# Four row transfers without waits between them, and gate dots at another rate

## The chip, the core and the metric

The kernel runs on one core of a Trainium2 chip. The metric is the device time of one execution in microseconds (us), so lower is better. The core has five engines, each with its own instruction stream: PE (TensorE, matmuls), ACT (ScalarE), DVE (VectorE), POOL (GpSimd) and SP (SyncE, which here only issues DMAs). An instruction can wait on semaphores that other engines or landed DMAs raise; everything behind it on its engine then waits too.

## The reference

Three stages follow one another. With S = 3072, D = 256 and 8 batches there are 24,576 tokens.

```
scores = z @ z.T / S;  attn = max(scores, 0)**2;  x = u * (attn @ v)           # attention, per batch
h = x @ w_in;  g = h * clip(h + 3, 0, 6) / 6;  x = g @ w_out                   # first MLP, d_ff = 2048
logits = x @ w_gate;  e = argmax(logits);  gate = softmax(logits)[e]           # routing, 8 experts
out = gate * sigmoid(x @ w_output_gate)[e] * (max(x @ w1[e], 0) @ w2[e])       # one expert of 8 per token
```

## The kernel before

Tokens are worked in 48 chunks q of 512, six (`NC`) to a batch. Each chunk passes an **A** block (attention: 24 units, one per 128 keys, `NJ`), and later an **M** block (first MLP: 16 units, one per 128 hidden features, `NF`). Blocks alternate: M(4), A(6), M(5), A(7) and so on up to M(45), A(47), then the M blocks that are left, then the experts (`E` units). All float32 products are made of high and low halves, so that one product is three matmuls.

The order is written out by hand. `run` walks over the units; for unit n it issues the scores or the first MLP matmul of a unit some places ahead (`stage1`), the split into halves two units ahead (`stage2`), and then `back`, the second matmul, which sums into the four PSUM banks `psx`. `when(step, fn)` hangs a side job on a step, behind that step's matmuls. A program step is no time: each engine runs its own list as far as its waits allow.

What matters here is what happens at the end of an M block. Its result for 512 tokens (four groups s of 128) stands in the four banks `psx`. The next block's `back` needs these banks, so PE may go on only after `evacuate` (ACT line 429, then DVE line 430) has copied each bank to `row[:, s]` in SBUF. There is one `row` tile for all chunks of this phase. During the next A and M blocks the chunk in `row` is routed: 32 **gate dots** on DVE (line 445, one per group and expert), the four `route` stages (lines 382 to 425; stage 4 ends with line 425), and then four **scatters** on POOL (line 434), indirect DMAs that send each token's row of 260 floats to its expert's region in HBM, `xs_d`. Only when scatter s has landed may the next chunk's `evacuate` write `row[:, s]`. `xs_d` is one tile, and each scatter counts as a write of the whole of it, so a scatter also waits until the one before it has landed.

`plan_chunk` sets the steps. m1 is the last unit of M(q), so the A block behind it spans m1+1 to m1+24 and the M block after that m1+25 to m1+40. Of a chunk with an A block behind it, `na` dots go into the A block at `ra` per unit, the rest into the following M block (line 677). n is the step behind the last dot; route stage 4 and the scatters stand at n+4. Chunks with (q+3) divisible by 6 have 26 dots in the A block, the others 18. The chunk's successor is evacuated behind m1+40. Of the chunks 4 to 45, which have an A block behind them, seven are of the 26-dot kind (9, 15, ..., 45).

On POOL, besides scatters, two subtractions per chunk (line 309, `xlt`, the low half of the MLP's input) run in the A block; in the expert phase POOL adds (line 636) and scatters results to `out` (line 639).

Of the kernel before, what the change touches and what calls it, by code (L numbers as in the profile page):

```python
# [8 lines left out]
F32 = mybir.dt.float32  # L9
# [18 lines left out]
def kernel(  # L28
# [17 lines left out]
    E = wcat.shape[0]  # L46
# [3 lines left out]
    NJ = S // P  # L50
    NF = DFF // P
    NC = S // TC
    NQ = B * NC
    NSUB = TC // P
# [15 lines left out]
    pe, act, dve, pool, sp = nc.tensor, nc.scalar, nc.vector, nc.gpsimd, nc.sync  # L70
# [6 lines left out]
    const = ctx.enter_context(tc.tile_pool(name="const", bufs=1))  # L77
# [9 lines left out]
    ident = const.tile([P, P], F32, name="ident")  # L87
    tri = const.tile([P, P], BF16, name="tri")
    ones = const.tile([P, P], BF16, name="ones")
    three = const.tile([P, 1], F32, name="three")  # L90
    ebias = const.tile([P, 1], F32, name="ebias")
    gbc = const.tile([P, E, D], F32, name="gbc")
# [54 lines left out]
    def when(step, fn, early=False):  # L147
        bg.setdefault((max(step, low[0]), not early), []).append(fn)
# [6 lines left out]
    def load_z(b, t):  # L155
        zr = ap.tile([P, TC], F32, tag="stage", name="zr", bufs=5)
        for h in range(2):
            sp.dma_start(out=zr[h * DQ:(h + 1) * DQ], in_=zT[b, :, t * TC:(t + 1) * TC])
        zraw[b, t] = zr
# [22 lines left out]
    def load_u(q):  # L182
        b, c = divmod(q, NC)
        t = mp.tile([P, ND, TC], F32, tag="xu", name="xut", bufs=2)
        sp.dma_start(out=t, in_=uT[b, :, c * TC:(c + 1) * TC].rearrange("(d p) t -> p d t", p=P))
        xu[q] = t
# [95 lines left out]
    def sum_o(q, d):  # L282
        if halves(q):
            t = ap.tile([P, TC], F32, tag="os", name="os", bufs=2)
            act.copy(t, o_t[q][2 * d + 1])  # L285
            dve.tensor_add(t, t, o_t[q][2 * d])
            osum[q, d] = t
        else:
            osum[q, d] = o_t[q][d]
            mul_x(q, d)  # L290

    def mul_x(q, d):
        if (q, d) in osum:
            dve.tensor_mul(xu[q][:, d, :], xu[q][:, d, :], osum.pop((q, d)))

    def split_x(q, d):
        if q in alt:
            if d == 0:
                alt[q] = pools["e"].tile([P, 2, ND, TC], F32R, tag="ws", name="xat", bufs=NPAIR + 2)
            h, l = (alt[q][:, k, d, :] for k in range(2))  # L300
        else:
            h = mp.tile([P, TC], F32R, tag="xph", name="xht", bufs=ND)
            l = mp.tile([P, TC], F32R, tag="xpl", name="xlt", bufs=ND)
        act.copy(h, xu[q][:, d, :])
        xh.setdefault(q, []).append(h)
        xl.setdefault(q, []).append(l)

    def split_xl(q, d):
        pool.tensor_sub(xl[q][d], xu[q][:, d, :], xh[q][d].bitcast(F32))

    def save_x(q):
        sp.dma_start(out=xsave[q], in_=xu.pop(q).rearrange("p d t -> p (d t)"))

    def reload_x(q):
        t = mp.tile([P, ND, TC], F32, tag="xu", name="xut", bufs=2)
        sp.dma_start(out=t, in_=xsave[q].rearrange("p (d t) -> p d t", d=ND))
        xu[q] = t
# [61 lines left out]
    def row_of(q):  # L379
        return pools["row"] if q in alt else row0  # L380
# [46 lines left out]
    def evacuate(q, s):  # L427
        o, row = o_t["x", q], row_of(q)
        act.activation(row[:, s, :D], o[s][:, :D], AF.Copy, scale=1.0 / 6.0)  # L429
        dve.scalar_tensor_tensor(row[:, s, :D], o[s][:, D:], 1.0 / 6.0, row[:, s, :D],  # L430
                                 op0=ALU.mult, op1=ALU.add)

    def scatter(q, s):
        pool.indirect_dma_start(  # L434
            out=xs_d,
            out_offset=bass.IndirectOffsetOnAxis(ap=rt["di", q][:, s:s + 1], axis=0),
            in_=row_of(q)[:, s, :],
            in_offset=None,
        )

    def gate_dot(q, k):
        s, e = divmod(k, E)
        if k == 0:
            rt["lg"] = rtile("lg", [P, NSUB, E])
        dve.tensor_tensor_reduce(junk, row_of(q)[:, s, :D], gbc[:, e, :], 1.0, 0.0, op0=ALU.mult, op1=ALU.add,  # L445
                                 accum_out=rt["lg"][:, s, e:e + 1])
# [50 lines left out]
    def table2a(stage):  # L497
        m, n, w = small["m"], stile("n2", 2 * E), stile("c")
        if stage == 0:
            ceil_div(n[:, E:], SLOT - 1)  # L500
        elif stage == 1:
            dve.tensor_sub(n[:, E:], n[:, E:], m[:, :E])
            p = prefix(n)
            dve.tensor_copy(tail[:, :E], base[0:1, :])
            dve.tensor_copy(tail[:, E:], p[0:1, 2 * E - 1:])
        elif stage == 2:
            dve.tensor_sub(w, m[:, :E], m[:, 1:])
            dve.tensor_add(w, w, n[:, E:])
        else:
            place(small["pa"], w, m[:, 0:1])  # L510

    def tableb(i):
        se = small["se"]
        w = TW[i]
        ps = ps_a()
        for j in range(2):
            mm(ps[0:1, j * w:(j + 1) * w], se[:, j:j + 1], ident[:, :w], True, True)
        dve.tensor_copy(tab[i][:, :2 * w], ps[0:1, :2 * w])
        dve.memset(tab[i][:, 2 * w:2 * w + 1], 1)
        dve.tensor_tensor(tab[i][:, 2 * w + 1:], tab[i][:, w + 1:2 * w], tab[i][:, w:2 * w - 1], op=ALU.not_equal)  # L520

    def fill_tail(e):
        r = nc.values_load(tail[0:1, e:e + 1], engines=(mybir.EngineType.SP,),
                           min_val=e * REG, max_val=e * REG + NT)
        sp.dma_start(out=xs_d[bass.ds(r, SLOT), :].rearrange("(a p) c -> p a c", p=P), in_=zrow)
# [131 lines left out]
    def plan_chunk(q):  # L657
        b, c = divmod(q, NC)
        s0, e0 = at["A", q, 0], at["A", q, NJ - 1]
        m0, m1 = at["M", q, 0], at["M", q, NF - 1]  # L660
        if q > 1:
            when(s0 + 4, lambda: load_u(q))
        for d in range(ND):
            when(e0 + 1, lambda d=d: sum_o(q, d))
            when(e0 + 2 + d, lambda d=d: mul_x(q, d))
        if q < NSAVE:
            when(e0 + 5, lambda: save_x(q))
            when(m0 - NF - 8, lambda: reload_x(q))
        sx = m0 - NF + 4 if q < NSAVE or q == NQ - 1 else m0 - NJ + 2
        for d in range(ND):  # L670
            when(sx + 2 * d, lambda d=d: split_x(q, d))
            when(sx + 2 * d + 1, lambda d=d: split_xl(q, d))
        kind = order[m1 + 1][0]
        if kind == "A":
            na, ra = (18, 0.85) if (q + 3) % NC else (26, 1.2)
            dots = [m1 + 2 + int(k / ra) for k in range(na)]
            dots += [m1 + NJ + 1 + int(k / 1.7) for k in range(NSUB * E - na)]
        else:
            rate = {"M": 3.0 if q else 1.0, "E": 0.5}[kind]
            d0 = m1 + 2 if kind != "E" else m1 + 22  # L680
            dots = [d0 + int(k / rate) for k in range(NSUB * E)]
        for k, step in enumerate(dots):
            when(step, lambda k=k: gate_dot(q, k))
        n = dots[-1] + 1
        for s in range(NSUB):
            when(m1 + 1, lambda s=s: evacuate(q, s))
        for st in range(1, 5):
            when(n + st - (st == 1), lambda st=st: route(q, st))
        sc = n + 4
        if q < NLATE:  # L690
            E0 = at["E", 0, 0]
            sc = max(E0 + 1, sc + (E0 + 1 - sc) % NPAIR)
        for st in range(NSUB):
            when(sc + (st * NPAIR if q < NLATE else 0), lambda st=st: scatter(q, st))
        if q == 1:
            for st in range(4):
                when(n + 6 + st, lambda st=st: table2a(st))
            when(n + 11, lambda: tableb(1))
            for e in range(E):
                when(sc + NPAIR * (NSUB + e), lambda e=e: fill_tail(e))  # L700
        if c == NC - 1 and b + 1 < B:
            for t in range(NZ):
                at_z = e0 + 1 + (5 * t) // 2
                when(at_z - 4, lambda t=t: load_z(b + 1, t))
                when(at_z, lambda t=t: prep_z(b + 1, t))
            for i in range(NV):
                at_v = e0 + 2 + (6 * i) // 5
                when(at_v - 3, lambda i=i: load_v(b + 1, i))
                when(at_v, lambda i=i: prep_v(b + 1, i))

    for q in range(NQ):
        plan_chunk(q)
# [152 lines left out]
```

## Time and profile before

| | |
|---|---|
| median of 3 runs | 5595.7 us (5592.58 to 5596.53) |
| profiled execution | 5592.97 us, its span 5590.8 us |
| PE busy | 5477.0 us (98%) |
| DVE busy | 4307.9 us (77%) |
| ACT busy | 3462.8 us (62%) |
| POOL busy | 904.1 us (16%) |
| mean granted TensorE clock | 0.989 |

PE is busy nearly all the time, so what counts is each stretch in which it stands still or runs slowly. Matmuls overlap in the trace (one of 512 columns shows some 400 ns, and starts follow one another every 230 ns or so), so a full-speed stretch and a half-speed stretch both look busy; the granted clock tells them apart.

### The profile page before, as it was taken

To read this page: it belongs to the slowest core of one execution; us is meant where nothing else is said; L and a number is where in the kernel's file an instruction comes from. 1 tells how busy PE (TensorE), PEld (TensorE's weight loads), DVE (VectorE), ACT (ScalarE), POOL (GpSimd) and SP (SyncE) were. 2 spreads that over 40 slices of the span, in tenths; PEclk is the share of its full clock that TensorE was granted. 3 is DMA by queue.
4 is the path that set the end of the run, shared out by engine and by line. 5 is a ranking of instruction groups with operands and counts; after the bars stand their busy time and mean duration, and the time that the engine had idled before them with its cause. 6 is when DMAs were issued, how large, how long until landed. Compare 5 with 4: busy or idle time off the path is not lost.

```text
span 5590.8 us, 97495 instructions
## 1 busy us (share of the span) xinstructions
PE 5477.0 (98%) x35672; PEld 4636.9 (83%) x35672; DVE 4307.9 (77%) x9967; ACT 3462.8 (62%) x5993; POOL 904.1 (16%) x782
## 2 busy tenths in 40 slices
PE   9999999999999999999999999999999999999999
PEld 6788778878887888788877888887888899999998
DVE  8977777777777777777777777777768888888887
ACT  7765566556655665565556555655554677777776
POOL 3200001000100000000000000100011244444443
PEclk9999999999999999999999999999999999999999
DMA  3110001000100000010001000100000122222233
GB/s 95 57 37 12 12 22 41 9 23 18 33 9 26 27 23 9 26 37 12 11 23 37 13 12 22 41 9 16 9 18 18 56 76 82 80 73 73 80 114 111
DMA packets 127381, 209.42 MB, mean 37 GB/s; under 512 B 15389, under 2 KB 84766, under 8 KB 126752
## 3 DMA queue, kind: packets, MB, share of 16 engines
q1 hardware_dynamic: 108064, 152.26, 9.4%
q0 software_dynamic: 18816, 50.75, 2.5%
q8 instruction: 281, 4.60, 0.3%
q14 instruction: 220, 1.80, 0.1%
HBM read 147.73 MB, written 56.27 MB: 36 GB/s over the span
## 4 chain that ended last, share of the span: by engine, by line
PE 75%; issue 12%; POOL 6%; DMA 4%; DVE 2%; ACT 1%; POOLq 0%; ACTq 0%; SPq 0%; DVEq 0%
PE psx L197 48%; PE psa L197 27%; POOL out L639 4%; DMA xs_d<-row,r_di 4%; POOL yt L636 1%; POOL xs_d L434 1%; DVE wst L581 0%; DVE row L430 0%; DVE lot L243 0%; ACT gt L231 0%; DVE gt L232 0%; ACT row L429 0%; PE psa L588 0%; DVE lot L611 0%; DVE junk L445 0%
## 5 line engine op out<-in xcount | busy, mean ns | idle before, releaser
L197 PE MATMUL psx<-hit,vht 64*128 64x512 f32 (+1 forms) x4320 | 1421.3, 403 | 91.6 <-DVE row L430 91.1
L197 PE MATMUL psx<-lot,vht 64*128 64x512 f32 (+1 forms) x4320 | 1413.0, 403 | 0.9 <-DVE lot L243 0.7
L197 PE MATMUL psx<-hit,vlt 64*128 64x512 f32 (+1 forms) x4320 | 1406.8, 402 | 0.0
L197 PE MATMUL psx<-wo,hit 128*128 128x512 f32 x3072 | 1114.0, 398 | 0.0
L231 ACT ACTIVATE gt<-psa,three 128x512 f32<-128x512 f32 x768 | 529.3, 689 | 890.2 <-PE psa L197 884.7
L197 PE MATMUL psa<-xht,win 128*128 128x512 f32 x2880 | 998.6, 394 | 0.0
L197 PEld LDWEIGHTS psx<-hit,vht 64*128 64x128 f32 (+1 forms) x4320 | 814.0, 189 | 221.6 <-DVE row L430 117.5
L219 ACT ACTIVATE at<-psa 128x512 f32<-128x512 f32 x1152 | 679.8, 590 | 375.9 <-PE psa L197 351.6
L243 DVE TENSOR_TENSOR lot<-at,hit 128x512 fp32r<-128x512 f32 x1152 | 816.2, 709 | 117.5 <-ACT hit L242 74.0
L197 PEld LDWEIGHTS psx<-hit,vlt 64*128 64x128 f32 (+1 forms) x4320 | 815.8, 190 | 92.2
L197 PEld LDWEIGHTS psx<-lot,vht 64*128 64x128 f32 (+1 forms) x4320 | 812.9, 190 | 85.7 <-DVE lot L243 2.0
L232 DVE SCALAR_TENSOR_TENSOR gt<-gt,psa 128x512 f32<-128x512 f32 x768 | 527.1, 686 | 443.2 <-ACT gt L231 430.5
L197 PE MATMUL psx<-wo,lot 128*128 128x256 f32 x3072 | 860.4, 280 | 0.0
L220 ACT ACTIVATE at<-at 128x512 f32<-128x512 f32 x1152 | 728.9, 633 | 36.7
L445 DVE CUSTOM_DVE_ANT_0 junk<-row,gbc 128x256 f32<-128x256 f32 x1536 | 736.3, 479 | 12.1
L434 POOL DMA_INDIRECT xs_d<-row,r_di x192 | 202.7, 1056 | 3297.3 <-DVE row L425 2955.5
L197 PEld LDWEIGHTS psx<-wo,hit 128*128 128x128 f32 x3072 | 577.0, 188 | 150.8 <-ACT at L219 15.5
L197 PEld LDWEIGHTS psa<-xht,win 128*128 128x128 f32 x2880 | 540.9, 188 | 138.0 <-ACT os L285 12.4
L197 PE MATMUL psa<-xht,wst 128*128 128x256 f32 x3200 | 649.7, 284 | 4.1 <-DVE wst L581 4.1
L197 PEld LDWEIGHTS psx<-wo,lot 128*128 128x128 f32 x3072 | 579.5, 189 | 25.4 <-DVE lot L243 0.4
L243 DVE TENSOR_TENSOR lot<-gt,hit 128x512 fp32r<-128x512 f32 x768 | 528.3, 688 | 83.4 <-ACT hit L242 83.4
L197 PE MATMUL psx<-wst,hit 128*128 128x512 f32 x1600 | 578.1, 395 | 0.0
(141 smaller groups left out, 9608.2 us busy)
## 6 DMA issues: line engine op xcount, KB each, us to landing
w<-in_wcat SPq DMA_DIRECT2D x64, 512.0 KB
x<-xs_d SPq DMA_DIRECT2D x100, 260.0 KB
vr<-in_v SPq DMA_DIRECT2D x96, 256.0 KB
xut<-in_uT SPq DMA_DIRECT2D x48, 512.0 KB
ogt<-in_w_ogT SPq DMA_DIRECT2D x100, 128.0 KB
zr<-in_zT SPq DMA_DIRECT2D x96, 128.0 KB
wraw<-in_w_in SPq DMA_DIRECT2D x16, 256.0 KB
wraw<-in_w_out SPq DMA_DIRECT2D x16, 256.0 KB
```

Source lines behind the costliest of these rows:

```text
L197: pe.matmul(o, l, r, start=start, stop=stop)
L219: act.activation(t, ps, AF.Relu, scale=1.0 / S)
L220: act.activation(t, t, AF.Square)
L231: act.activation(t, ps, AF.Relu, bias=three)
L232: dve.scalar_tensor_tensor(t, t, 6.0, ps, op0=ALU.min, op1=ALU.mult)
L243: dve.tensor_sub(l, t, h.bitcast(F32))
L434: pool.indirect_dma_start(out=xs_d, out_offset=bass.IndirectOffsetOnAxis(ap=rt["di", q][:, s:s + 1], axis=0), in_=row_of(q)[:, s, :], in_o ...
L445: dve.tensor_tensor_reduce(junk, row_of(q)[:, s, :D], gbc[:, e, :], 1.0, 0.0, op0=ALU.mult, op1=ALU.add, accum_out=rt["lg"][:, s, e:e + 1])
L636: pool.tensor_add(y[:, 0, :], y[:, 0, :], y[:, 1, :])
L639: ins = pool.indirect_dma_start(out=out, out_offset=bass.IndirectOffsetOnAxis(ap=x.bitcast(I32)[:, s, D + 1:D + 2], axis=0), in_=y[:, 0, : ...
```

## The change

Two edits. The scatter is put in a group of writers of `xs_d` that do not depend on one another, and a memset of one element on POOL stands before each. The dots of chunks of the 18-dot kind go 20 into the A block at 0.95 per unit; the rest of both kinds starts one unit later in the M block and goes 2.2 per unit instead of 1.7.

```diff
+    spacer = const.tile([1, 1], F32, name="spacer")
...
     def scatter(q, s):
-        pool.indirect_dma_start(
+        pool.memset(spacer, 0.0)
+        ins = pool.indirect_dma_start(
             out=xs_d,
             out_offset=bass.IndirectOffsetOnAxis(ap=rt["di", q][:, s:s + 1], axis=0),
             in_=row_of(q)[:, s, :],
             in_offset=None,
-        )
+        ).ins
+        tc.declare_no_dep(ins, group="xs", reason="each token has a row of its own")
+        tc.add_to_no_dep_group("xs", ins)
...
-            na, ra = (18, 0.85) if (q + 3) % NC else (26, 1.2)
+            na, ra = (20, 0.95) if (q + 3) % NC else (26, 1.2)
             dots = [m1 + 2 + int(k / ra) for k in range(na)]
-            dots += [m1 + NJ + 1 + int(k / 1.7) for k in range(NSUB * E - na)]
+            dots += [m1 + NJ + 2 + int(k / 2.2) for k in range(NSUB * E - na)]
```

On POOL, the four scatters of one chunk and the subtractions behind them stood like this before (a `DMASW` name is a semaphore that landed indirect DMAs raise, eight of them in turn; `DVE_49` is DVE's):

```order
L434 DMA xs_d<-row_82,r_di 198912x260 [waits DMASW3_49,DVE_49]
L434 DMA xs_d<-row_82,r_di 198912x260 [waits DMASW4_49]
L434 DMA xs_d<-row_82,r_di 198912x260 [waits DMASW5_49]
L434 DMA xs_d<-row_82,r_di 198912x260 [waits DMASW6_49]
L309 TENSOR_TENSOR xlt<-xut,xht 128x512 [waits DMAHW5_49,PE_49,Activation_49]
```

and stand like this now (lines are one to four numbers higher, and `row_83` is the same tile):

```order
L435 MEMSET spacer 1x1 [waits Pool_49]
L436 DMA xs_d<-row_83,r_di 198912x260 [waits DMASW0_49,DVE_49]
L435 MEMSET spacer 1x1 [waits Pool_49]
L436 DMA xs_d<-row_83,r_di 198912x260 [waits DMASW1_49]
L435 MEMSET spacer 1x1 [waits Pool_49]
L436 DMA xs_d<-row_83,r_di 198912x260 [waits DMASW2_49]
L435 MEMSET spacer 1x1 [waits Pool_49]
L436 DMA xs_d<-row_83,r_di 198912x260 [waits DMASW3_49]
L310 TENSOR_TENSOR xlt<-xut,xht 128x512 [waits DMAHW0_49,PE_49,Activation_49]
```

Before, each scatter waited for the semaphore of the scatter just ahead of it. Now the semaphore it waits for is its own, which the scatter eight places ahead (two chunks earlier) raised; the first eight scatters of the program, which have none ahead, carry no such wait.

On DVE, the end of an M block stood like this before, from route stage 4 (`r_sm`, then line 425) to the first split of the next block (`hit<-at`); a `gt`, `lot` pair is one M unit:

```order
L232 SCALAR_TENSOR_TENSOR gt<-gt,psa 128x512
L243 TENSOR_TENSOR lot<-gt,hit 128x512
L424 TENSOR_REDUCE r_sm<-r_d 128x4
L425 TENSOR_SCALAR row_82<-r_sm 128x4
L232 SCALAR_TENSOR_TENSOR gt<-gt,psa 128x512
L243 TENSOR_TENSOR lot<-gt,hit 128x512 x2
L240 CAST hit<-at 128x512
```

and now:

```order
L233 SCALAR_TENSOR_TENSOR gt<-gt,psa 128x512
L244 TENSOR_TENSOR lot<-gt,hit 128x512
L425 TENSOR_REDUCE r_sm<-r_d 128x4
L426 TENSOR_SCALAR row_83<-r_sm 128x4
L233 SCALAR_TENSOR_TENSOR gt<-gt,psa 128x512
L244 TENSOR_TENSOR lot<-gt,hit 128x512
L233 SCALAR_TENSOR_TENSOR gt<-gt,psa 128x512
L244 TENSOR_TENSOR lot<-gt,hit 128x512 x2
L241 CAST hit<-at 128x512
```

Route stage 4, which releases the scatters, has moved ahead by one M unit in chunks of the 18-dot kind. In the seven chunks of the 26-dot kind it moves back by one, since their last dot goes from step m1+27 to m1+28. In the expert phase nothing moves but the memsets ahead of the eight scatters of chunks 0 and 1.

## Rows read from the trace of the kernel before

**Rows 1.** The page's busy time by engine: us, share of the span, instructions.

```profile
PE 5477.0 (98%) x35672; PEld 4636.9 (83%) x35672; DVE 4307.9 (77%) x9967; ACT 3462.8 (62%) x5993; POOL 904.1 (16%) x782
```

**Rows 2.** Groups by line and form: busy us, mean ns | idle us before, releasers.

```profile
L197 PE MATMUL psx<-hit,vht 64*128 64x512 f32 x4032 | 1303.5, 402 | 91.1 <-DVE row L430 91.1
```

**Rows 3.** Waits: waiter <- waited for: us in total, times, longest.

```profile
POOL xs_d L434 <- DMA xs_d<-row,r_di: 248.1, 122, 3.8
...
ACT row L429 <- DMA xs_d<-row,r_di: 115.7, 59, 2.9
...
PE psx L197 <- DVE row L430: 91.1, 62, 2.8
```

**Rows 4.** Timeline of POOL at M(13)'s end: start, us, what, [idle before <- releaser].

```profile
1137.34 0.99 POOL L434 DMA_INDIRECT xs_d<-row,r_di  x1 [72.51 <-DVE row L425]
...
1142.92 1.37 POOL L434 DMA_INDIRECT xs_d<-row,r_di  x1 [1.76 <-DMA xs_d<-row,r_di]
1146.72 0.96 POOL L434 DMA_INDIRECT xs_d<-row,r_di  x1 [2.43 <-DMA xs_d<-row,r_di]
```

**Rows 5.** Timeline of ACT, the same place: first two and last evacuation.

```profile
1143.90 0.75 ACT L429 ACTIVATE row<-psx 128x256 f32<-128x256 f32 x2
...
1149.25 0.38 ACT L429 ACTIVATE row<-psx 128x256 f32<-128x256 f32 x1 [2.33 <-DMA xs_d<-row,r_di]
```

**Rows 6.** Timeline of PE, the same place: its two pauses.

```profile
1147.43 0.49 PE L197 MATMUL psx<-hit,vht 64*128 64x512 f32 x1 [0.91 <-DVE row L430]
1150.15 0.79 PE L197 MATMUL psx<-hit,vht 64*128 64x512 f32 x1 [2.22 <-DVE row L430]
```

**Rows 7.** Timeline of POOL before M(10)'s end: last scatter of chunk 9 (26-dot kind).

```profile
863.87 1.45 POOL L434 DMA_INDIRECT xs_d<-row,r_di  x1 [2.64 <-PE psa L197]
```

**Rows 8.** Timeline of ACT at M(10)'s end: its four evacuations.

```profile
871.46 1.19 ACT L429 ACTIVATE row<-psx 128x256 f32<-128x256 f32 x4
```

**Rows 9.** Windows: stretch: us, busy us (x) of PE, PEld, DVE, ACT, POOL, PEclk, DMA.

```profile
1150.00:1156.40 6.40, 6.25 (x30) 4.92 (x32) 6.19 (x15) 4.62 (x9) 1.28 (x1) 0.52 0.00 0
1156.40:1175.00 18.60, 18.60 (x164) 15.97 (x162) 14.88 (x40) 12.86 (x23) 1.29 (x1) 1.00 0.11 30
```

**Rows 10.** The core's span and its mean granted TensorE clock.

```profile
core 0: 5590.8 us, clock 0.989
```

**Rows 11.** Timeline of PE: first scores behind M(5), M(10), M(11), M(45).

```profile
412.18 0.50 PE L197 MATMUL psa<-zht 64*128 64x512 f32 x2
...
871.97 0.50 PE L197 MATMUL psa<-zht 64*128 64x512 f32 x2
...
959.83 0.50 PE L197 MATMUL psa<-zht 64*128 64x512 f32 x2
...
4076.97 0.50 PE L197 MATMUL psa<-zht 64*128 64x512 f32 x2
```

**Rows 12.** Timeline of POOL: the program's last scatter, right behind another.

```profile
5581.74 0.98 POOL L639 DMA_INDIRECT out<-yt,x  x1 [0.30 <-issue]
```

**Rows 13.** Groups by line and form: a gate dot; a memset of 128x8.

```profile
L445 DVE CUSTOM_DVE_ANT_0 junk<-row,gbc 128x256 f32<-128x256 f32 x1536 | 736.3, 479 | 12.1
...
L654 POOL MEMSET row<- 128x8 f32 x1 | 0.1, 103 | 0.0
```

**Rows 14.** Timeline of DVE late in M(13): two successive units.

```profile
1135.47 0.69 DVE L232 SCALAR_TENSOR_TENSOR gt<-gt,psa 128x512 f32<-128x512 f32 x1 [0.81 <-ACT gt L231]
...
1138.26 0.69 DVE L232 SCALAR_TENSOR_TENSOR gt<-gt,psa 128x512 f32<-128x512 f32 x1 [1.19 <-ACT gt L231]
```

**Rows 15.** Timeline of all engines in A(12), unit 5: POOL's subtraction, a dot, `lot`, its matmul.

```profile
878.47 1.37 POOL L309 TENSOR_TENSOR xlt<-xut,xht 128x512 fp32r<-128x512 f32 x1 [1.14 <-ACT xht L304]
...
878.61 1.52 DVE L445 CUSTOM_DVE_ANT_0 junk<-row,gbc 128x256 f32<-128x256 f32 x1
...
880.50 0.69 DVE L243 TENSOR_TENSOR lot<-at,hit 128x512 fp32r<-128x512 f32 x1
...
881.53 0.39 PE L197 MATMUL psx<-lot,vht 64*128 64x512 f32 x1
```

## The prediction

> **What bounds the kernel now.** I read the page's busy times first: PE is at 98%, the next engine at 77% [rows 1], so time can come only from PE's idle stretches or from stretches in which it runs slowly. The groups by line show where PE idles: of some 114 us (span less busy time), 91.1 lie in front of one group, the matmuls that begin an A block's `back`, and all of it ends with DVE line 430, the evacuation of the block before [rows 2]. The list of waits gives the chain behind it: that matmul waits for DVE line 430, whose ACT partner, line 429, waits 59 times, 115.7 us in all, for a scatter to land, and a scatter waits 122 times, 248.1 us, 2.03 on the mean, for the scatter ahead of it [rows 3].
>
> The timeline shows one case, the end of M(13), where chunk 12 is scattered. The first scatter starts at 1137.34, when route stage 4 releases it. The others each wait some 1.8 to 2.4 us for the landing of the one ahead, so the last starts at 1146.72 and ends at 1147.68 [rows 4]. ACT evacuates groups 0 and 1 at 1143.90, but group 3 only at 1149.25, 2.33 us late, when that scatter has landed [rows 5]. PE pauses 0.91 and then 2.22 us [rows 6].
>
> Where the scatters are early, nothing pauses: chunk 9, with 26 dots in its A block, issues its last one at 863.87 [rows 7], 7.6 us before the evacuation at 871.46, which then runs as four copies in a row [rows 8].
>
> The clock adds to this. Behind M(13)'s pause the granted clock is 0.52 for 6.4 us, that is, almost at 1.2 instead of 2.4 GHz, and then 1.00 again [rows 9]. PE works in that stretch, at half its pace. Over the program the mean is 0.989 [rows 10].
>
> **What one boundary costs.** Of the 42 M blocks that are followed by an A block, the first has no scatter ahead of it and six follow a 26-dot chunk. That leaves 35, and 91.1 / 35 = 2.60 us of pause each. I price all of it, clock included, in two ways.
>
> First, pause and clock apart. Half clock costs half the time it lasts, so the mean clock says (1 - 0.989) x 5590.8 = 61.5 us lost in all [rows 10], and 91.1 + 61.5 = 152.6 us. A little of the 61.5 lies elsewhere.
>
> Second, by period. From the scores behind M(10) to those behind M(11), a period with no pause, it is 959.83 - 871.97 = 87.86 us. The 40 periods from M(5) to M(45) take 4076.97 - 412.18 = 3664.79 [rows 11], against 40 x 87.86 = 3514.4. The excess of 150.4 is that of 34 pauses, 4.42 each, so 35 cost 154.8. The two agree, and I take 153 us as what all 35 boundaries have to give.
>
> **The scatters without waits.** In the order, no scatter waits for its neighbour now, only for the one eight places earlier, two chunks or some 180 us before. So the four run at POOL's own pace. A scatter takes 0.96 to 0.99 us by itself and up to 1.37 here [rows 4]. The program's last scatter to `out` doesn't wait for the landing of the one ahead: it starts 0.30 us behind that one's end and takes 0.98 [rows 12]. The new memset isn't in the trace; the nearest row, 128x8 elements, is 0.10 us [rows 13], and one element should be no more. Its floor is nothing, its ceiling the 0.30 us that ends up between two such scatters [rows 12]. I take 0.97 + 0.10 = 1.07 us as the pitch, with 1.07 as well as 1.37 + 0.30 = 1.67 kept as ends. The last of four then ends 4 x 1.07 = 4.3 us after the first starts (6.7 at most) instead of 10.3, and lands about 2.03 later, at 6.3 (8.7 at most).
>
> By row 4's start of 1137.34 that is 1143.6 (1146.0 at most). ACT wants group 3 about 0.8 us after group 0, at 1144.7. So this edit alone takes away the wait for group 3 on the expected pace, and leaves 1.3 us of it on the slowest. Most of that stays hidden: with some 0.4 us each on ACT and DVE, group 3's bank is then free at 1146.8, and PE's pause at that place began at 1147.43 - 0.91 = 1146.5 [rows 6].
>
> One rule speaks against this. The third scatter takes 1.37 us where others take 0.96 [rows 4]. The Trainium skill (SBUF — State Buffer, Who interferes with whom) says that GpSimd is shut out of its port pair for as long as VectorE runs a copy or cast in a 2-port mode, and that a DMA's descriptors aren't written meanwhile. By it every scatter that meets a cast takes those 0.4 us more, 1.6 for four, which is inside the slowest pace above.
>
> **The dots.** For the 18-dot chunks the order shows route stage 4 one M unit earlier; a unit is 1138.26 - 1135.47 = 2.79 us [rows 14]. The scatters start at about 1134.5, and the last lands at 1140.8 (1143.2 at most), before ACT asks for any group. That is the margin that makes 35 of 35 likely. The scatters also leave the stretch in which DVE casts for the next A block. The seven 26-dot chunks start theirs 2.79 later. They had 7.6 us from the last scatter's start to the evacuation, serially, and need 1 + 2 of it, so this costs nothing.
>
> The price is on DVE. 35 chunks do 20 dots instead of 18 in the A block and 12 instead of 14 in the M block: the sum is the same. What can hurt is where they stand. In the A block the thin place is unit 5: two dots meet POOL's subtractions, one of them taking 1.52 us, and `lot` is ready at 880.50 + 0.69 = 881.19 for a matmul at 881.53, 0.34 us to spare [rows 15]. Up to there old and new rates put one dot on the same six units (k / 0.85 and k / 0.95 both give 0 to 5 for k = 0 to 5). The seventh comes one unit earlier, behind the thin place, and a dot there takes well under DVE's gain per unit. So PE stays covered, at 0.34 us; a dot of about 0.5 us in front of unit 5 would cost up to 0.2 us and perhaps a clock drop.
>
> In the M block three dots meet in one unit, 3 x 0.48 = 1.4 us [rows 13] beside `gt` and `lot` at 0.69 each [rows 14, 15] and one more product of that size (`xut`), 3.5 against a unit of 2.79. DVE falls behind by 0.7 once, having had no dot in the unit before, and `lot` is made two units (5.6 us) ahead of its use. I cost it at nothing.
>
> POOL's extra work is 192 memsets, 20 us on an engine that is busy 16% [rows 1], hidden everywhere. In the expert phase 8 of them stand in front of scatters of which each is a slot apart.
>
> **The sum.** The profiled execution of 5592.97 us less 153 gives 5440. The median of the three runs lies 2.7 above that execution, so I forecast 5443 us for the median, 2.7% less.
>
> **Rivals.**
>
> *The transfers still follow one another.* If the 2.03 us between scatters were the time for which the DMA engines are taken, and not how long a landing is reported after it, dropping the wait changes nothing and only the dots help: the chain moves 2.79 earlier. M(13)'s last evacuation would come at 1146.5 instead of 1149.25 and PE pause 0.7 us instead of 3.1; at 0.5 on the mean 35 x 0.5 = 18 us come back, without the clock about 5461, and with it (35 x 1.7) about 5520. The last scatter to `out`, which takes 0.98 us with another in flight, speaks against it [rows 12], though it shows the issue and not the landing. The Trainium skill (DMA: Bandwidth & Descriptors, Anatomy of one DMA) puts a fixed 2.0 us on such a transfer and says that it is mostly the wait for the write's receipt, which would let four overlap; the 2.03 of rows 3 agrees in size.
>
> *DVE is the next to be late.* With the pause gone, DVE loses the time in which it caught up, and unit 5 of the A block, 0.34 us from PE [rows 15], could slip behind in the 35 blocks. At 0.1 to 0.5 us each that is 4 to 18 us, and with half the clock drops some 30 more: 5447 to 5490. Against it: behind M(10) there is no pause either, the same first six dots, and PE doesn't wait.
>
> *Slower: four transfers in flight spoil one another.* They write 512 scattered rows to HBM at once. Slower than before begins where the last lands more than 12.3 + 2.79 = 15.1 us after the first starts, where 12.3 is today's serial chain (10.3 + 2.03) and 2.79 the earlier start. At 18 us each boundary pauses 2.9 us longer, 35 x 2.9 = 102, so about 5700. Nothing in the trace has four in flight; it would need each transfer to be four times as slow as alone.
>
> **Chances and range.** The forecast 0.81, follow one another 0.07, DVE late 0.08, slower 0.02, something else 0.02, half of it about no change. The forecast's own range is 5435 to 5452: the two pricings, the 4 us by which runs differ, and a few boundaries that keep a rest. To it I add DVE late and the better half of the first rival: 5428 to 5490, the low end for pauses elsewhere that go along. About 0.2% (11 us) is what a measurement of this kernel can tell from no change; faster by more than that 0.96, within it 0.015, slower 0.025.
>
> **What would show it.** Right: four scatters of a chunk within 5 us, the wait of ACT line 429 for a landing near 0, no idle in front of the first `psx<-hit,vht`, a period of 87.9 us everywhere, and a mean clock of 0.998 or more. Wrong in the transfers: ACT line 429 still waits for landings. Wrong in the dots: PE waits for `lot` (line 244 now) in units 5 to 8 of A blocks. Wrong in the clock: pauses gone and the mean still near 0.99, which would give 5592.97 - 91 = 5502.

## The result and the profile after

The changed kernel takes 5426.1 us (median of four runs, three of them 5424.8 to 5426.7) against 5596.05 (5592.58 to 5596.53) for the kernel before: a ratio of 0.9697, 95% interval 0.9678 to 0.9716. (The fourth run, 7698 us at a mean granted clock of 0.64, is left out of the ratio.) Its profiled execution took 5425.52 us. The forecast was 5443 with a range of 5428 to 5490, so the direction was right, and the time lies 1.9 us below the range.

First the page, by which [rows 1, 2 and 10] are answered: busy time by engine and the granted clock in 40 slices.

```profile
PE 5401.3 (100%) x35672; PEld 4558.2 (84%) x35672; DVE 4287.1 (79%) x9967; ACT 3463.7 (64%) x5993; POOL 914.5 (17%) x974
...
PEclk9999999999999999999999999999999999999999
```

The groups by line and form have the matmuls that had 91.1 us of idle time in front of them [rows 2]:

```profile
L198 PE MATMUL psx<-hit,vht 64*128 64x512 f32 x4032 | 952.2, 392 | 0.0
```

The core's span and clock [rows 10]:

```profile
core 0: 5423.3 us, clock 0.999
```

The idle time is gone, and with it the slow stretches: the trace's clock record has 33 stretches at half clock before, 129.4 us together, the last of them (9.95 us) behind the program's last matmul, and after only that last one, 8.7 us. The list of waits no longer has ACT's evacuation waiting for a landing, nor PE's matmuls for DVE line 431 (430 before). Of [rows 3] two successors are left, the time that POOL spends on nothing in sight between two scatters, and a short wait for DVE line 431 by PE's weight loads (PEld on the page, one for each matmul):

```profile
POOL xs_d L436 <- issue: 31.4, 144, 0.4
...
PEld psx L198 <- DVE row L431: 2.1, 9, 0.4
```

What M(13)'s end looks like now is seen on POOL's timeline (start, us, what, idle time before), answering [rows 4]:

```profile
1103.10 0.98 POOL L436 DMA_INDIRECT xs_d<-row,r_di  x1 [69.24 <-DVE row L426]
1104.09 0.09 POOL L435 MEMSET spacer<- 1x1 f32 x1
1104.39 0.96 POOL L436 DMA_INDIRECT xs_d<-row,r_di  x1 [0.21 <-issue]
...
1106.91 0.96 POOL L436 DMA_INDIRECT xs_d<-row,r_di  x1 [0.23 <-issue]
```

on ACT's [rows 5],

```profile
1112.44 1.44 ACT L430 ACTIVATE row<-psx 128x256 f32<-128x256 f32 x4
```

and on PE's, [rows 6]:

```profile
1113.39 0.50 PE L198 MATMUL psa<-zht 64*128 64x512 f32 x2
...
1114.19 0.41 PE L198 MATMUL psx<-hit,vht 64*128 64x512 f32 x2
```

Four scatters take 4.8 us instead of 10.3 and end at 1107.9; ACT copies the four groups without a break, 4.6 us later; PE goes from the last matmul of M(13) through the scores into `back` without a pause.

Last, the periods, from PE's first scores behind one M block to those behind the next (M(5), M(10), M(11), M(12), M(45)), answering [rows 11]:

```profile
412.80 0.50 PE L198 MATMUL psa<-zht 64*128 64x512 f32 x2
...
850.56 0.50 PE L198 MATMUL psa<-zht 64*128 64x512 f32 x2
...
938.39 0.50 PE L198 MATMUL psa<-zht 64*128 64x512 f32 x2
...
1025.89 0.50 PE L198 MATMUL psa<-zht 64*128 64x512 f32 x2
...
3916.48 0.50 PE L198 MATMUL psa<-zht 64*128 64x512 f32 x2
```

The 40 periods take 3503.68 us against 3664.79, 161.1 less. The period behind M(10) is 87.83 and that behind M(11) 87.50. So the pause-free period of before that served as a yardstick, 87.86 [rows 11], was of a longer kind.

### The profile page after: what moved, and what is told of

It is laid out like the page before. It is cut to its first block, busy times and chain, and to the rows that moved or that the text cites. A ratio compares the mean times of both kernels' runs of the same rounds, so it can differ in the third digit from the quotient of the medians.

```text
span 5423.3 us, 97689 instructions
## 1 busy us (share of the span) xinstructions
PE 5401.3 (100%) x35672; PEld 4558.2 (84%) x35672; DVE 4287.1 (79%) x9967; ACT 3463.7 (64%) x5993; POOL 914.5 (17%) x974
## 4 chain that ended last, share of the span: by engine, by line
PE 78%; issue 14%; POOL 8%; DVE 0%; DMA 0%; POOLq 0%; ACT 0%; SPq 0%; DVEq 0%; ACTq 0%
PE psx L198 50%; PE psa L198 28%; POOL out L643 6%; POOL yt L640 2%; POOL xs_d L436 0%; DMA x<-xs_d 0%; POOLq L643 0%; POOLq L640 0%; DMA zr<-in_zT 0%; DMA out<-yt,x 0%; DVE wst L585 0%; DVE hit L241 0%; DVE lot L244 0%; PE psa L592 0%; DVE row L431 0%
## 5 line engine op out<-in xcount | busy, mean ns | idle before, releaser
L198 PE MATMUL psx<-hit,vht 64*128 64x512 f32 (+1 forms) x4320 | 1070.6, 393 | 0.5 <-DVE hit L241 0.5
L198 PE MATMUL psx<-lot,vht 64*128 64x512 f32 (+1 forms) x4320 | 1069.5, 394 | 0.5 <-DVE lot L244 0.5
L198 PE MATMUL psx<-hit,vlt 64*128 64x512 f32 (+1 forms) x4320 | 1069.5, 394 | 0.0
L449 DVE CUSTOM_DVE_ANT_0 junk<-row,gbc 128x256 f32<-128x256 f32 x1536 | 716.5, 466 | 12.1
L198 PEld LDWEIGHTS psx<-hit,vht 64*128 64x128 f32 (+1 forms) x4320 | 561.1, 185 | 115.3 <-DVE hit L241 3.7
L198 PEld LDWEIGHTS psx<-hit,vlt 64*128 64x128 f32 (+1 forms) x4320 | 561.0, 185 | 95.9
L198 PEld LDWEIGHTS psx<-lot,vht 64*128 64x128 f32 (+1 forms) x4320 | 560.5, 185 | 96.0 <-DVE lot L244 1.4
```

The source lines that it names most:

```text
L198: pe.matmul(o, l, r, start=start, stop=stop)
```

## The experiments

What was open after the result: which of the two edits brings the gain, why it is 14.5 us larger than forecast, and whether the half clock really is a consequence of the pauses. The theory that stood at the end: waits among scatters made the last landing late, PE paused for it, longer than its idle time shows, and a pause of that size halves the clock behind it; so whatever gets the last scatter landed before the evacuation gives all of the gain. Against it stood that the moved dots bring part of the gain by themselves, and that something else in the chain of transfers slowed PE. Each expectation says what its theories give. Four runs share one set of runs of the kernel before (5591.73 us, 5588.67 to 5593.78); the last three share another (5590.23 us, 5588.91 to 5593.64).

**The group alone (e1_group_only).** The changed kernel with the dots of before.

```diff
-            na, ra = (20, 0.95) if (q + 3) % NC else (26, 1.2)
+            na, ra = (18, 0.85) if (q + 3) % NC else (26, 1.2)
-            dots += [m1 + NJ + 2 + int(k / 2.2) for k in range(NSUB * E - na)]
+            dots += [m1 + NJ + 1 + int(k / 1.7) for k in range(NSUB * E - na)]
```

> The scatters' group and memsets as in the changed kernel, the dots at the old rates. Theory A (the whole gain is the 35 pauses and the half-clock stretches behind them; the forecast was short because the pause-free period of 87.86 us that it used is of a longer kind, and because idle is counted from modelled matmul ends): the scatters start at the old place, 6.8 us before the evacuation, follow one another every 1.27 us and have all landed when group 3 is wanted. No pause, period 87.50 us behind 18-dot chunks, about 5426 us (5422 to 5430). Theory B (the other dot rates make each A and M block shorter by themselves): pauses gone, but the period stays 87.86, about 5436. Theory C (the earlier start is needed): pauses of some 0.3 us at the 35 places remain, 5437 without clock drops.

Measured: 5425.32 us, ratio 0.9703 (0.9687 to 0.9719), span 5423.1, clock 0.999. POOL's timeline at M(13)'s end, then ACT's:

```profile
1105.82 0.98 POOL L436 DMA_INDIRECT xs_d<-row,r_di  x1 [72.02 <-DVE row L426]
...
1109.64 0.96 POOL L436 DMA_INDIRECT xs_d<-row,r_di  x1 [0.22 <-issue]
```

```profile
1112.37 1.44 ACT L430 ACTIVATE row<-psx 128x256 f32<-128x256 f32 x4
```

The scatters stand 2.7 us later and still end 1.8 us before ACT's first copy; with 2.0 us for the landing (e5_late_2, below) the last is there before ACT takes the fourth group at about 1113.4. The spans agree within 0.2 us: with the group, the second edit is worth nothing, and it costs nothing. That the dots add a share to what the group brings is refuted for this kernel. No run has the group without its memset or the memset without the group, so what the memset does, beside its 0.09 us on POOL, is not shown.

**The dots alone (e2_dots_only).** The kernel before with the new dots, the scatters still one after another.

```diff
-            na, ra = (18, 0.85) if (q + 3) % NC else (26, 1.2)
+            na, ra = (20, 0.95) if (q + 3) % NC else (26, 1.2)
-            dots += [m1 + NJ + 1 + int(k / 1.7) for k in range(NSUB * E - na)]
+            dots += [m1 + NJ + 2 + int(k / 2.2) for k in range(NSUB * E - na)]
```

> The new dot rates, the scatters as before, each waiting for the landing of the one ahead. Theory A: the serial chain starts 2.79 us earlier and is as long as before, so group 3's scatter lands about 1.6 us later than wanted, and PE pauses 0.7 to 0.9 us at the 35 places, 28 us in all: about 5454 if so short a pause leaves the clock alone, about 5514 if each drops it for 3.4 us. Theory B (the dot rates shorten the blocks): some 10 us less than either. If the waits among the scatters were not what cost the time, it would be near 5426.

Measured: 5444.91 us, ratio 0.9737 (0.9721 to 0.9754), span 5442.5, clock 0.999. So 2.79 us of earlier start gives most of the gain as well. What is left, 19.2 us of span over 35 boundaries, is 0.55 each, and the list of waits hardly shows it: POOL waits as before, ACT a little, PE next to nothing.

```profile
POOL xs_d L434 <- DMA xs_d<-row,r_di: 258.3, 130, 3.9
...
ACT row L429 <- DMA xs_d<-row,r_di: 19.2, 19, 2.4
...
PE psx L197 <- DVE row L430: 4.9, 7, 2.0
```

PE's 4.9 us are a quarter of the 19.2 that it lost. The clock is no answer here, as it stays at 0.999. So PE's idle time in this view is too small; how much, e5_late_2 tells. The same list has the weight loads that go ahead of these matmuls, and they show nearly all of it:

```profile
PEld psx L197 <- DVE row L430: 21.0, 42, 2.5
```

Less the 2.1 us of the changed kernel that is 18.9 of the 19.2.

**The thin place on DVE (e4_dense_dots).** The changed kernel with the 20 dots packed closer, so that in A(15) five of them instead of three stand ahead of unit 5's `lot`, two of these right in front of it.

```diff
-            na, ra = (20, 0.95) if (q + 3) % NC else (26, 1.2)
+            na, ra = (20, 1.5) if (q + 3) % NC else (26, 1.2)
```

> The changed kernel with the 20 dots of the A block at 1.5 per unit instead of 0.95, so that two or three more of them stand in front of unit 5. This prices the thin place of the A block, where DVE makes `lot` 0.78 us (0.33 behind a 26-dot chunk) before PE uses it. Expected: DVE 0.9 to 1.4 us later there, PE pauses 0.1 to 0.6 us in each of the 35 blocks, 5430 to 5447 us without clock drops, up to 5500 with them. If DVE's rate did not matter there: 5426, no pause.

Measured: 5435.95 us, ratio 0.9722 (0.9706 to 0.9738), span 5433.8, clock 0.999. DVE's timeline ahead of unit 5 in A(15), and PE's at that unit:

```profile
1122.30 1.52 DVE L449 CUSTOM_DVE_ANT_0 junk<-row,gbc 128x256 f32<-128x256 f32 x1
...
1123.86 0.43 DVE L449 CUSTOM_DVE_ANT_0 junk<-row,gbc 128x256 f32<-128x256 f32 x1
...
1124.67 0.69 DVE L244 TENSOR_TENSOR lot<-at,hit 128x512 fp32r<-128x512 f32 x1
```

```profile
1124.76 0.40 PE L198 MATMUL psx<-hit,vlt 64*128 64x512 f32 x2
1124.99 0.39 PE L198 MATMUL psx<-hit,vht 64*128 64x512 f32 x2
1125.41 0.49 PE L198 MATMUL psx<-lot,vht 64*128 64x512 f32 x2
1125.75 0.40 PE L198 MATMUL psx<-hit,vlt 64*128 64x512 f32 x2
```

`lot` is ready at 1125.36 and its matmul starts at 1125.41, 0.42 behind the one ahead, where the normal step is 0.23; the next step is 0.34 instead of 0.23. That is 0.19 + 0.11 = 0.30, and 35 periods are 0.29 longer or so (35 x 0.29 = 10.2 of the 10.5 us of span). No idle time stands beside these rows, since the matmul ahead still shows as running until 1125.38. In the changed kernel, with two dots less ahead, the same `lot` and its matmul stand like this, DVE's row and PE's:

```profile
1121.36 0.69 DVE L244 TENSOR_TENSOR lot<-at,hit 128x512 fp32r<-128x512 f32 x1
```

```profile
1122.83 0.40 PE L198 MATMUL psx<-lot,vht 64*128 64x512 f32 x2
```

There 1122.83 - 1122.05 = 0.78 us are left: DVE was near its limit, but the change didn't use it up.

**Scatters two units later (e5_late_2).** The changed kernel with the M block's dots two units later, which puts the scatters near the evacuation.

```diff
-            dots += [m1 + NJ + 2 + int(k / 2.2) for k in range(NSUB * E - na)]
+            dots += [m1 + NJ + 4 + int(k / 2.2) for k in range(NSUB * E - na)]
```

> The changed kernel with the dots of the M block two units later, so that the four scatters, still without waits among them, start 5.6 us later. Theory A: the last lands 2 us later than wanted, PE pauses 1.2 to 1.4 us at the 35 places, 45 us: about 5471 without clock drops, about 5530 with one of 3.4 us behind each. This tells, with the dots alone, from which pause the clock falls. If landings set nothing, 5426.

Measured: 5466.21 us, ratio 0.9776 (0.9759 to 0.9792), span 5464.2, clock 0.999. At M(13)'s end, POOL, ACT and PE:

```profile
1119.49 0.96 POOL L436 DMA_INDIRECT xs_d<-row,r_di  x1
...
1120.76 0.96 POOL L436 DMA_INDIRECT xs_d<-row,r_di  x1
```

```profile
1120.71 0.75 ACT L430 ACTIVATE row<-psx 128x256 f32<-128x256 f32 x2
1122.06 0.38 ACT L430 ACTIVATE row<-psx 128x256 f32<-128x256 f32 x1 [0.60 <-DMA xs_d<-row,r_di]
1123.72 0.38 ACT L430 ACTIVATE row<-psx 128x256 f32<-128x256 f32 x1 [1.28 <-DMA xs_d<-row,r_di]
```

```profile
1121.66 0.50 PE L198 MATMUL psa<-zht 64*128 64x512 f32 x2
...
1123.18 0.39 PE L198 MATMUL psx<-hit,vht 64*128 64x512 f32 x1
1124.62 0.50 PE L198 MATMUL psx<-hit,vht 64*128 64x512 f32 x1 [1.04 <-DVE row L431]
...
1124.96 0.61 PE L198 MATMUL psx<-hit,vlt 64*128 64x512 f32 x2
...
1210.70 0.50 PE L198 MATMUL psa<-zht 64*128 64x512 f32 x2
```

Three readings. The last two of the four transfers are landed 2.00 us (1120.76 + 0.96 to 1123.72) and 1.61 us (1119.49 + 0.96 to 1122.06) behind their instructions, when ACT may go on; alone it was 1.57 to 2.43 [rows 4, 5]. So no slowing shows where transfers overlap. Four are not in flight at once here, though: from start to landing it is 2.6 to 3.0 us, and one starts every 1.27, so two overlap, for moments three. The pause shows as 1.04 us, but the period, 1210.70 - 1121.66 = 89.04, is 1.54 longer than 87.50. The rows say where the 0.5 is: two matmuls of this form start together (x2 in [rows 11] and at 28 of the 42 boundaries in the profile after), so the second one was due at 1123.19 and came at 1124.62, 1.43 late, of which 0.39 is covered by the first one, shown as running; and the next pair starts 0.34 behind instead of 0.23. 1.43 + 0.11 = 1.54. And behind this pause the clock does not fall, as the window shows (us, busy of five engines, granted clock, DMA):

```profile
1125.00:1131.40 6.40, 6.40 (x58) 5.49 (x56) 6.26 (x12) 5.83 (x11) 2.91 (x3) 1.00 0.01 3
```

Over the program, PE idles 44.0 us (5464.2 less 5420.2 busy), 22.0 more than in the changed kernel, and loses some 1.7 to the clock (half of one stretch of 3.4 us, which lies behind none of the 35 boundaries); the span is 40.9 longer. 17.2 us, 0.49 at each of 35 boundaries, stand in no idle time of PE. The weight loads' waits have them, 39.0 more than in the changed kernel:

```profile
PEld psx L198 <- DVE row L431: 41.1, 54, 1.5
```

That reading is better, not perfect: in e4_dense_dots the weight loads wait 16.6 us more for `lot` (line 244), and the span is only 10.5 longer.

**Three units later (e6_late_3).** One unit more.

```diff
-            dots += [m1 + NJ + 2 + int(k / 2.2) for k in range(NSUB * E - na)]
+            dots += [m1 + NJ + 5 + int(k / 2.2) for k in range(NSUB * E - na)]
```

> The changed kernel with the second part of every chunk's dots three M units later, so that route stage 4 and the four scatters come one unit (2.79 us) later than in e5_late_2, where each boundary was 1.15 us longer than in the changed kernel. By either theory each of 35 boundaries then lasts 1.15 + 2.79 = 3.94 us longer, and the scatters still don't wait for one another. Theory 'a long pause of PE halves the clock behind it, whatever caused the pause': the granted clock falls behind most of the 35 pauses, as it did in the kernel before, some 1.75 us lost each time (61.5 / 35), mean clock about 0.989, 5426 + 35 x (3.94 + 1.75) = 5625 us. Rival 'the clock fell for something that only the kernel before did (its chain of transfers), not for the pause': no drops, mean clock 0.999, 5426 + 35 x 3.94 = 5564 us.

Measured: 5629.49 us, ratio 1.0068 (1.0051 to 1.0085), 0.7% slower than the kernel before; span 5627.4, clock 0.984. PE's timeline and a window at M(13)'s end:

```profile
1155.28 0.49 PE L198 MATMUL psx<-hit,vht 64*128 64x512 f32 x1 [0.55 <-DVE row L431]
1156.84 0.49 PE L198 MATMUL psx<-hit,vht 64*128 64x512 f32 x1 [1.06 <-DVE row L431]
...
1159.05 0.49 PE L198 MATMUL psx<-hit,vht 64*128 64x512 f32 x1 [0.65 <-DVE row L431]
```

```profile
1159.60:1163.07 3.47, 3.47 (x20) 2.70 (x18) 3.37 (x8) 2.84 (x6) 1.28 (x1) 0.51 0.00 0
```

Here PE comes late to all four banks, with idle time in front of three, and then works at half clock. The clock record has such a stretch behind each of the 35 late boundaries, and behind none of the other seven. The scatters never wait for one another in this kernel. So the half clock needs no chain of transfers, it follows long pauses for late landings, and the rival (5564) falls. How the 204.1 us over the changed kernel divide is less sure than their sum. By half of the record's slow stretches the clock took 2.44 us per boundary (85.5 / 35) instead of 1.75, and the pauses 3.39 instead of 3.94; but some of these stretches lie under the pauses. By the weight loads' waits the pauses took 3.94, as expected (130.1 us for DVE line 431, 2.1 in the changed kernel, and 10.0 more with no releaser in sight), and the clock 1.89.

**26 dots for every chunk, scatters one after another (e7_26_dots).** The kernel before with one line changed.

```diff
-            na, ra = (18, 0.85) if (q + 3) % NC else (26, 1.2)
+            na, ra = 26, 1.2
```

> The kernel before, its scatters still waiting for one another, with 26 dots at 1.2 per unit in the A block for every chunk, so that all chunks scatter as early as chunk 9 does. Theory 'a scatter's wait for its neighbour costs nothing where the chain ends before the evacuation': no pauses, ACT's evacuations wait for no landing, mean clock 0.999. How long the periods then are tells apart what made the seven periods behind 26-dot chunks 87.84 us in the changed kernel where the others were 87.50: if the 26 dots in the A block did, all periods are 87.8 or more and the time is about 5426 + 35 x 0.34 = 5438 us; if the change of batch did, which falls on the same blocks, the 35 others stay at 87.50 and the time is 5425 to 5427. If the waits among scatters cost something by themselves, as on POOL's subtractions behind them, pauses stay and the time is above 5445.

Measured: 5426.8 us, ratio 0.9707 (0.9691 to 0.9723), span 5423.2, clock 0.999. POOL and ACT at M(13)'s end, and PE's first scores behind M(12) and M(13):

```profile
1091.67 0.98 POOL L434 DMA_INDIRECT xs_d<-row,r_di  x1 [58.30 <-DVE row L425]
...
1100.00 0.96 POOL L434 DMA_INDIRECT xs_d<-row,r_di  x1 [1.94 <-DMA xs_d<-row,r_di]
```

```profile
1112.16 1.44 ACT L429 ACTIVATE row<-psx 128x256 f32<-128x256 f32 x4
```

```profile
1025.62 0.50 PE L197 MATMUL psa<-zht 64*128 64x512 f32 x2
...
1113.12 0.50 PE L197 MATMUL psa<-zht 64*128 64x512 f32 x2
```

POOL still waits 255.6 us for landings, and nothing is lost, since at M(13) the last scatter ends 11 us ahead of the evacuation. And the period is 87.50 behind a 26-dot chunk here too: the seven longer periods are not made by the dots.

**20 dots for every chunk (e8_all_20).** The changed kernel without the exception.

```diff
-            na, ra = (20, 0.95) if (q + 3) % NC else (26, 1.2)
+            na, ra = 20, 0.95
```

> The changed kernel with 20 dots at 0.95 per unit in the A block for the seven 26-dot chunks too. If the 26 dots made their periods (and the one ahead of each) longer, by 0.34 and 0.27 us, those seven pairs fall to 87.50 and the time is 5426 - 7 x 0.61 = 5421.7 us. If the change of batch made them longer, the time stays at 5426, or rises by some us where DVE, with more dots in an M block that also begins a batch, falls behind.

Measured: 5425.53 us, ratio 0.9705 (0.9688 to 0.9721), span 5423.3, the changed kernel's own. The same seven periods are 87.83 to 87.87 here, and those just ahead of them 87.77 to 87.79. They fall where a batch ends, with as many matmuls (586) as the others and no idle time of PE in sight. Set side by side start by start, the matmuls of the long period behind M(10) and of the short one behind M(11) part at one place, the second matmul of the A block's `back`, and the 0.33 us between them stay the same from there to the end of the M block. It is a small pause for the evacuation, and the kernel before has it too. These are DVE's and PE's rows there at M(10), where the yardstick of [rows 11] begins:

```profile
872.23 1.41 DVE L430 SCALAR_TENSOR_TENSOR row<-psx,row 128x256 f32<-128x256 f32 x4
```

```profile
872.79 0.74 PE L197 MATMUL psx<-hit,vht 64*128 64x512 f32 x2
```

DVE begins to evacuate 0.26 us behind the first scores (871.97), where at M(13) it begins 0.34 ahead of them (1144.51 against 1144.85). So the two matmuls of the first pair, shown as one row, start some 0.25 apart, and the row is 0.74 long where an undisturbed pair shows 0.41. The seven longest periods in the changed kernel begin with such a pair, 0.25 apart, and those just ahead of them with one 0.20 apart. Shortly before M(10)'s end DVE splits a part of the next batch's v (line 179, 0.68 us at 869.36), which it doesn't do at M(13). That this makes DVE late fits the size, but no run took it away.

Little is left to gain by moving dots and scatters: four kernels end within 0.2 us of one span, and PE, busy 5401.3 of 5423.3 us, has 22 us of idle left, over a quarter of it ahead of the program's first matmul.

## Why the prediction came out as it did

**What bounds the kernel: right.** All 35 pauses went, and nothing took their place.

**What one boundary costs: the step that failed, by its size.** 153 us were put down as all that 35 boundaries had to give; they gave nearly all of 167.5 (span 5590.8 to 5423.3). The mechanism was right, the term 14.5 short. Both ways of pricing were short, for reasons of their own, and their agreement was taken for a proof; that they met within 2.2 us was chance. The first point needs one row of the waits of before:

```profile
PEld psx L197 <- DVE row L430: 118.2, 79, 3.1
```

- Pause and clock apart: 91.1 + 61.5 counted idle time of the matmuls as the trace shows it. As e5_late_2 and e2_dots_only show, a pause is some 0.5 us longer than that, and the weight loads' waits come nearer. Before, they were 118.2 us, against 2.1 now, so by this estimate the pauses took 116.1 where 91.1 was put down, 25 more. That leaves 51.4 of the 167.5 for the clock, 10 less than 61.5: of the record's 129.4 us at half clock, 9.95 lie behind the last matmul and some under the pauses, and neither costs anything. So two errors stood against each other, and the larger won.
- By period: the yardstick of 87.86 was taken as one with no pause, and had one of 0.3 us at the change of batch (e8_all_20). 40 x 87.86 = 3514.4 stood for what became 3503.68, and 10.7 of the gain was left out. With the right yardstick it is 161.1 over 34 boundaries, 4.74 each and 165.8 for 35, 1.7 short of what came. The sign of being right that asked for 87.9 everywhere was wrong with it: 28 of the 40 periods are 87.50 or 87.59.

All periods of before without a wait for landings, the one behind M(4) aside, were behind 26-dot chunks, which could be read in the kernel; that these stand at the same places as the change of batch, too.

A smaller term was off the same way: 2.7 us were added from the profiled execution to the median, and that difference came out at 0.6.

**The scatters without waits: right.** The pitch is 1.27 us (0.96, the memset 0.09, 0.21 of nothing in sight) where 1.07 was taken and 1.67 was the end. The 0.30 us between two scatters [rows 12] was taken as a ceiling for the memset; it came out as the whole gap, memset and nothing in sight together. None of it reaches PE. That the edit alone takes away the wait for group 3 was right too (e1_group_only).

The rule of the Trainium skill (SBUF — State Buffer, Who interferes with whom) on VectorE's casts and GpSimd was held against the change. The changed kernel's scatters at M(13) meet no cast and take 0.96 to 0.98 us. Where one met a cast, the last of e2_dots_only, it took 1.42; in e5_late_2 one that met a cast near its end took 0.96, and the memset behind it 0.26 instead of 0.09. So the 0.4 us appear, but not each time, and that the cast causes them is not shown.

**The dots: cost right, worth overrated.** They cost nothing, as said; the margin that was to make 35 of 35 likely was not needed (e1_group_only). That a further dot ahead of unit 5 would cost up to 0.2 us was near: two more cost 0.29, without a clock drop.

**The rivals.** Transfers that follow one another: fallen, as each scatter starts before the one ahead of it is landed, 1.6 to 2.0 us behind its instruction. That agrees with what the Trainium skill (DMA: Bandwidth & Descriptors, Anatomy of one DMA) says, that most of the fixed 2 us is the wait for the receipt. The rival's own price was good, though: the chain moved by 2.79 was to leave 18 us, and e2_dots_only, which is that case, keeps 18.8 over the changed kernel (5444.9 to 5426.1). DVE late: fallen for the dots; at the thin place of A(15) 0.78 us are to spare. DVE's late evacuation at the change of batch was there before and has stayed. Spoiling one another: nothing of it shows in e5_late_2's landings, where two or three transfers overlap; four at once, which the rival took for granted, were not put to the test.

**The range.** Its low end was explained by pauses elsewhere. It should have come from the two prices themselves: one was open to what the matmuls' idle time doesn't show, the other to what the yardstick might hold, and both of these only add to the gain.

## What to carry to other kernels

A chain of transfers that follow one another costs nothing as long as its last landing comes before the buffer is wanted; starting it early enough (e7_26_dots) and letting it overlap (e1_group_only) are two ways to one result, here to 0.2 us, so try the cheaper one first. Price a pause of PE by the distance between starts, against a place where nothing pauses, not by the matmuls' idle time, and look at the weight loads' waits beside it; and see that the undisturbed place differs from the disturbed ones in nothing but the pause. When two estimates agree, ask whether both err to the same side.

## What the runs showed of the hardware

- A pause of PE shows about 0.5 us too short in the matmuls' idle time when they go in pairs (1.04 shown, 1.54 lost in e5_late_2), and one of 0.3 us doesn't show at all (e4_dense_dots). The weight loads' waits show nearly all of it in two runs (39.0 of 40.9 us in e5_late_2, 18.9 of 19.2 in e2_dots_only), and too much in e4_dense_dots (16.6 for 10.5).
- Short pauses left the clock alone: 35 of about 1.15 us each kept it at 0.999 (e5_late_2). Boundaries at which PE stood still for some 3.3 us in all (116.1 / 35, by the weight loads) dropped it to half at 31 of 35 places before, and those of e6_late_3, where PE paused several times with a little work between, at all 35.
- Indirect scatters that one engine issues every 1.27 us, so that two or three overlap, are landed 1.6 to 2.0 us behind their instructions (e5_late_2, M(13)), as one alone is (1.57 to 2.43).
